# The order of the work of a linear-attention and gated-FFN kernel, laid out anew behind its first 148 entries

## The chip, the cores and the metric

The kernel runs on one core of a Trainium2 chip. The metric is the time of one execution on the device in microseconds (us). Besides the plain runs there is one profiled execution, from which all rows of the profile are.

## What is computed

Eight batches, eight heads, 576 positions, head width 64. For each batch and head the attention has no softmax: k and v are multiplied into a 64x64 matrix, q times that matrix is the output, and the output is scaled by its root mean square over the head width. The heads side by side are the 512 columns of x. Then comes a feed-forward layer with 1024 hidden columns: a ReLU, a convolution of three taps over the positions, a sigmoid of it as a gate, and a product with the output matrix.

```python
kv = np.einsum('bhsd,bhse->bhde', k, v)
out = np.einsum('bhsd,bhde->bhse', q, kv)
rms = np.sqrt(np.mean(out * out, axis=-1, keepdims=True) + 1e-06)
x = out / rms * g_norm
h = np.maximum(x @ w_in, 0.0)
# conv_out[s] = w0 * h[s - 1] + w1 * h[s] + w2 * h[s + 1], per column
out = (h * gate) @ w_out        # gate = 1 / (1 + exp(-conv_out))
```

## The kernel before, in words

All work is cut into small operations, and a list of 852 entries (ORDER) says in which order they are issued. An entry is a name with its numbers; behind an @ stands a slot: the bank of PSUM that it writes (of eight; two neighbouring banks for most), or the place in a ring of buffers in SBUF. `om.1.2.0.4@4` is the operation `om` for pair 1, row block 2, with four hidden blocks from 0 on, in bank 4. A loop at the end of the kernel runs the list from front to back, and a last pass ties each instruction to the one before it on its engine. So every engine works strictly in the list's order, and between engines only data and the reuse of banks and buffers make one wait. A bank may be written again when its last reader is done: an entry on the matmul engine (PE) with a slot may thus wait for a copy on VectorE (DVE) or ScalarE (ACT).

The work of a batch b goes like this. `Lq`, `Lk`, `Lv` load q, k and v (L348, on the queue of GpSimd, POOL). `kv` (or `kz`) multiplies k and v (L403, L480), `kva` or `kvd` copies the result to SBUF on ACT (L417) or on DVE (L415), one function with two names. `qt` transposes q on PE (L434) and `qd` copies it (L444); batches 6 and 7 are transposed by DMA instead (`tq`, L468), and `kx` moves halves of their kv matrix to the other partitions. `ot` (or `ox`) multiplies q by kv (L461, L501). For batches 0 to 3, `sq` squares it on ACT (L510), `on` or `oq` sums the squares on PE (L529, L538), `nl` takes the reciprocal root on ACT (L546), and `mo` scales on DVE into x (L557). For batches 4 to 7, `oc` copies the output to SBUF on ACT (L522), `ss` sums the squares of two batches into a few rows (L567), `ln` takes the root (L575), `sl` splits the result on DVE into parts (L582 to L585), `sp` spreads them over the partitions on PE (L594), and `mu` scales on DVE (L600).

The hidden layer is `hk`, `hs` or `hm` on PE (L659, L629, L614) with its ReLU on ACT: `rp`, `rh`, `re` (L666, L641, L620). Then `ta` makes two tap products on DVE (L682, L683), `aa` and `ab` add them (L688, L693), `sg` is the sigmoid on ACT (L699), and `mg` multiplies the gate in (L723); for four hidden blocks of batch 0, `cv` does the convolution on PE (L709) and `sc` the sigmoid (L716). `fi` are matmuls of zeros in the first 28 us. The output is `om` (`oh` for half rows) on PE (L733, L758), eight hidden blocks for a row block of 128, issued in two halves of four; `ea` copies it out of PSUM on ACT (L739), `ed` on DVE (L744), `eh` and `dh` do it for half rows, and `st` and `sh` store it from the queue of SyncE (SP).

Before an ACT operation that needs another table of functions stands a load (L228). `sg` and `sc` use one table, `nl` and `ln` the other.

The array of PE is used in several tiles: whole (128x128) for `hk`, `hs`, `hm`, `on`, `om` and `oh`, in 64x64 quarters for `kv`, `kz`, `qt`, `ot`, `ox` and `oq`, as 128x32 for `ss`, and as 32x128 for `sp`.

Of the kernel before, what the change touches and what calls it, by code (L numbers as in the profile page):

```python
# [76 lines left out]
hk.1.7.1.0@1 hk.1.5.1.1 rh.1.2.1 rh.1.0.1 rh.1.6.1 qt.2.0.0@4 rh.1.3.1 qt.2.1.0@2 Lq.5.0.4@2 sg.0.1.5 qd.2.0.0@0
sg.0.1.4 qd.2.1.0@1 ab.0.1.3 hk.1.4.1.0@6 hk.1.4.1.1 hk.1.1.0.0@7 hk.1.1.0.1 hk.1.5.0.0@4 hk.1.7.0.0@5 hk.1.0.0.0@2
hk.1.0.0.1 mg.0.1.2 rh.1.1.0 rh.1.4.1 rh.1.0.0 sg.0.1.6 ta.1.1.1@0 ta.1.1.0 aa.1.1.0 hk.1.7.1.1 hk.1.2.0.0@3
hk.1.5.0.1 hk.1.6.0.0@7 hk.1.7.0.1 hk.1.4.0.0@2 hk.1.4.0.1 hk.1.6.0.1 om.0.1.0.4@6 hk.1.2.0.1 rh.1.7.1 sg.0.1.7  # L80
rh.1.5.1 kv.2.0.2@0 rh.1.4.0 rh.1.5.0 rh.1.2.0 rh.1.6.0 kva.2.0.2@0 rh.1.7.0 om.0.2.0.4@2 mg.0.1.3 ab.1.1.0 om.0.1.4.4
# [10 lines left out]
hs.2.7.1@4 hs.3.7.0@5 qd.5.0.0@2 qd.4.1.0@3 sg.1.1.4 sg.1.1.5 hs.3.0.0@6 mg.1.1.2 ta.1.1.6@1 hs.3.3.1@0 ta.1.1.7
aa.1.1.3 hs.3.2.1@1 hs.3.2.0@7 rh.2.3.0 rh.2.6.0 rh.3.3.1 sg.1.1.3 rh.3.7.0 rh.3.2.1 rh.2.7.1 rh.3.0.0 sg.1.1.2
kv.4.0.2@2 hs.3.3.0@0 hs.3.6.0@1 kvd.4.0.2@0 ab.1.1.3 qt.5.1.0@2 ot.4.0.0@4 hs.3.0.1@6 rh.3.3.0 rh.3.2.0 rh.3.6.0
mg.1.1.1 hs.3.7.1@0 hs.3.1.0@1 hs.3.5.0@7 qd.5.1.0@4 ta.2.2.2@0 hs.3.4.0@2 om.0.7.0.4@3 sg.1.1.6 sg.1.1.7 rh.3.0.1
# [730 lines left out]
```

## Time and profile before

| | us |
|---|---|
| median of 3 runs | 177.63 |
| lowest and highest | 177.57 and 177.76 |
| the profiled execution | 177.69 |
| its span, first to last instruction | 175.8 |

The granted clock of TensorE is 0.999 of full speed in the profiled execution. PE is the matmul engine, PEld its weight loads, L733 is line 733 of the kernel. A row of a timeline has the start, the time until the last of the instructions merged in it ends, engine, line, operation and operands, and in brackets how long the engine was idle before it and what ended that. A row of the chain has start, length, and engine with what it wrote and the line. A row of stretches has the stretch, its length, and each engine's busy time in it.

### The profile page before, as it was taken

To read this page: it belongs to the slowest core of one execution; us is meant where nothing else is said; L and a number is where in the kernel's file an instruction comes from. 1 tells how busy PE (TensorE), PEld (TensorE's weight loads), DVE (VectorE), ACT (ScalarE), POOL (GpSimd) and SP (SyncE) were. 2 spreads that over 40 slices of the span, in tenths; PEclk is the share of its full clock that TensorE was granted. 3 is DMA by queue.
4 is the path that set the end of the run, shared out by engine and by line. 5 is a ranking of instruction groups with operands and counts; after the bars stand their busy time and mean duration, and the time that the engine had idled before them with its cause. 6 is when DMAs were issued, how large, how long until landed. Compare 5 with 4: busy or idle time off the path is not lost.

```text
span 175.8 us, 5059 instructions
## 1 busy us (share of the span) xinstructions
PE 168.3 (96%) x2091; PEld 100.3 (57%) x2110; DVE 146.6 (83%) x286; ACT 150.7 (86%) x272; POOL 22.5 (13%) x35
## 2 busy tenths in 40 slices
...
GB/s 162 392 321 206 207 205 208 208 208 207 208 208 210 280 209 205 128 208 232 227 240 255 60 0 0 167 121 134 60 63 0 0 20 159 123 159 181 124 190 125
DMA packets 25911, 29.10 MB, mean 165 GB/s; under 512 B 6037, under 2 KB 20385, under 8 KB 25889
## 3 DMA queue, kind: packets, MB, share of 16 engines
...
## 4 chain that ended last, share of the span: by engine, by line
PE 71%; ACT 18%; DVE 5%; DMA 3%; issue 3%; ACTq 0%
PE banks L733 30%; PE banks L629 12%; PE banks L659 8%; PE banks L614 5%; ACT taps L699 5%; ACT h L641 3%; DMA stg<-in_v_dram 3%; ACT sq L510 2%; ACT h L620 2%; PE banks L434 2%; PE banks L709 2%; PE banks L461 2%; PE banks L403 2%; PE banks L529 2%; PE banks L287 1%
## 5 line engine op out<-in xcount | busy, mean ns | idle before, releaser
L733 PE MATMUL banks<-w_out_sb,h 128*128 128x512 bf16 x265 | 62.9, 380 | 0.9 <-issue 0.3
L733 PEld LDWEIGHTS <-h 128*128 128x128 bf16 x280 | 26.1, 98 | 30.1 <-issue 1.0
L699 ACT ACTIVATE taps<-taps,cw 128x576 bf16<-128x576 bf16 (+1 forms) x44 | 40.3, 963 | 3.0 <-DVE taps L693 2.8
L629 PE MATMUL banks<-x,w_in_sb 128*128 128x288 bf16 (+2 forms) x256 | 33.8, 286 | 0.0
L641 ACT ACTIVATE h<-banks 128x288 bf16<-128x288 f32 (+2 forms) x80 | 29.5, 475 | 0.5 <-PE banks L659 0.5
L629 PEld LDWEIGHTS <-w_in_sb 128*128 128x128 bf16 x256 | 24.4, 98 | 7.1 <-issue 0.2
L723 DVE TENSOR_TENSOR h<-h,taps 128x1152 bf16<-128x1152 bf16 (+1 forms) x24 | 22.8, 952 | 1.0 <-ACT taps L699 0.9
L510 ACT ACTIVATE sq<-banks 128x576 bf16<-128x576 f32 (+2 forms) x32 | 20.7, 704 | 1.3 <-PE banks L461 1.0
L688 DVE TENSOR_TENSOR taps<-taps 128x1152 bf16<-128x1152 bf16 (+1 forms) x22 | 21.4, 974 | 0.4
L693 DVE TENSOR_TENSOR taps<-taps,h 128x1152 bf16<-128x1152 bf16 (+1 forms) x22 | 21.3, 970 | 0.2
L739 ACT ACTIVATE row<-banks 128x512 f32<-128x512 f32 x25 | 14.6, 595 | 5.1 <-issue 2.2
L682 DVE TENSOR_SCALAR taps<-h,cw 128x576 bf16<-128x576 bf16 (+1 forms) x44 | 18.8, 426 | 0.3 <-ACT h L641 0.3
L683 DVE TENSOR_SCALAR taps<-h,cw 128x576 bf16<-128x576 bf16 (+1 forms) x44 | 18.5, 421 | 0.0
L659 PE MATMUL banks<-x,w_in_sb 128*128 128x288 bf16 (+2 forms) x128 | 17.7, 286 | 0.1
L557 DVE SCALAR_TENSOR_TENSOR x<-banks,cw,rs 128x576 bf16<-128x576 f32 (+2 forms) x16 | 13.0, 814 | 5.0 <-ACT rs L546 5.0
L614 PE MATMUL banks<-x,w_in_sb 128*128 128x288 bf16 x128 | 16.7, 286 | 0.1
L614 PEld LDWEIGHTS <-w_in_sb 128*128 128x128 bf16 x128 | 12.3, 98 | 4.0
L659 PEld LDWEIGHTS <-w_in_sb 128*128 128x128 bf16 x128 | 12.2, 98 | 4.1 <-DMA w_in_sb<-in_moe_w_in_dram 0.2
L228 ACT ACT_TABLE_LOAD x10 | 12.8, 1283 | 2.0 <-issue 1.8
L444 DVE COPY qT<-banks 128x1152 bf16<-128x1152 bf16 (+2 forms) x13 | 8.7, 681 | 5.5 <-PE banks L434 5.4
L600 DVE SCALAR_TENSOR_TENSOR x<-o,cw,banks 128x576 bf16<-128x576 f32 (+2 forms) x16 | 11.9, 808 | 1.0 <-PE banks L594 1.0
L546 ACT ACTIVATE rs<-banks,eps_sb 128x576 f32<-128x576 f32 (+2 forms) x16 | 11.8, 740 | 0.7 <-PE banks L529 0.6
...
## 6 DMA issues: line engine op xcount, KB each, us to landing
...
```

Of the source, the lines that this page charges most:

```text
L510: nc.scalar.activation(T["sq", b, u, s], T["o", b, u, s], AX.Square)
L614: nc.tensor.matmul(ps[:, s, :HS], w_in_sb[:, t, f * P:(f + 1) * P], T["x", b][:, t, c0:c1], start=(t == 0), stop=(t == NT - 1))
L629: nc.tensor.matmul(ps, w_in_sb[:, t, f * P:(f + 1) * P], T["x", b][:, t, c0:c1], start=(t == 0), stop=(t == NT - 1))
L641: nc.scalar.activation(h, fr, AX.Relu)
L659: nc.tensor.matmul(T[at], w_in_sb[:, t, f * P:(f + 1) * P], T["x", b][:, t, c0:c1], start=(t == 0), stop=(t == NT - 1))
L682: nc.vector.tensor_scalar_mul(tap[:, 0, f % 2, :n, 8:8 + S], h[:, f], cw[:, f:f + 1])
L683: nc.vector.tensor_scalar_mul(tap[:, 1, f % 2, :n, :S], h[:, f], cw[:, 2 * NF + f:2 * NF + f + 1])
L688: nc.vector.tensor_add(tap[:, 1, :, :n, :S], tap[:, 0, :, :n, 7:7 + S], tap[:, 1, :, :n, 1:1 + S])
L693: nc.vector.tensor_add(y, y, span(b, n)[:, 2 * j:2 * j + 2])
L699: nc.scalar.activation(y, y, AX.Sigmoid, scale=cw[:, NF + f:NF + f + 1])
L723: nc.vector.tensor_mul(h, h, tap_of(b, j)[:, 1, :, :n, :S])
L733: nc.tensor.matmul(T["om", p, m], h[:, f, m * P:(m + 1) * P], w_out_sb[:, f, :], start=(f == 0), stop=(f == NF - 1))
```

## The change

From entry 149 on the list is laid out again. It has 852 entries as before, and nearly the same ones: `kva.2.0.2` and `kva.3.0.2` become `kvd`, the copies out of PSUM change their engine in `om.0.1`, `om.1.8`, `om.2.0` and `om.3.4` (from DVE to ACT) and in `om.1.6`, `om.1.7`, `om.3.5` and `om.3.6` (from ACT to DVE), and `eh.3.8.1` becomes `dh.3.8.1`. Most other entries move by a few places, and many get other slots. The kernel also gains operations that the list doesn't use (`ff`, `dw`, `df`, `mr`, `ad`, and `y_of` for `ad`); what `on` and `oq` write is put in one bank where both halves fit, which is so for the tiles of 256 columns of batch 0 alone.

Of the list, the parts that are spoken of:

```diff
-rh.3.1.0 sq.4.0.0@0 rh.3.5.0 rh.3.7.1 mg.1.1.3 ot.4.0.1@6 ta.2.2.0@1 ta.2.2.1 Lv.5.0.4@1 oc.4.0.0@0 Lk.5.0.4@0
-rh.3.4.0 kv.5.0.2@0 ot.4.1.0@4 om.0.7.4.4 oc.4.0.1@1 sq.4.0.1@1 kvd.5.0.2@1 ta.2.2.3 ot.5.0.0@0 ed.0.7@4 aa.2.2.1
-aa.2.2.0 ot.4.1.1@6 hs.2.7.0@2 oc.4.1.0@2 sq.4.1.0@2 ot.5.0.1@4 om.0.8.0.4@3 om.0.8.4.4 sq.5.0.0@3 oc.5.0.0@3
-sq.5.0.1@4 rh.2.7.0 oc.5.0.1@4 ot.5.1.1@0 ot.5.1.0@4 oc.4.1.1@5 sq.4.1.1@5 om.0.5.0.4@2 om.0.5.4.4 sq.5.1.1@6
-sq.5.1.0@7 ss.4.4.2@6 ss.5.4.2 ln.4@0 ab.2.2.1 ed.0.8@5 Lv.6.0.4@0 Lk.6.0.4@1 om.0.4.0.4@3 om.0.4.4.4 kz.6.0.2@6
-Lq.7.0.4@1 oc.5.1.0@6 oc.5.1.1@7 om.0.6.0.4@4 ab.2.2.0 ed.0.5@3 ea.0.4@0 sl.4@0 sg.2.2.2 sp.4.0.0.4@0 sp.4.1.1.4@2
-kvd.6.0.2@0 mu.4.1.1@2 om.0.6.4.4 sp.4.1.0.4@2 mu.4.0.0 sp.4.0.1.4@6 st.0.7 hs.2.6.1@5 mu.4.0.1 mu.4.1.0 hs.3.5.1@0
-st.0.5 ea.0.6@1 kx.6@0 sp.5.1.0.4@6 rh.2.6.1 ox.6.0.0@4 Lk.7.0.4@0 Lv.7.0.4@1 tq.6.1@0 st.0.4 st.0.3 st.0.8 st.0.6
-tq.7.0@2 tq.7.1@3 rh.3.5.1 mu.5.1.0@0 sp.5.1.1.4@0 hm.4.7@2 sp.5.0.1.4@6 mu.5.1.1 oc.6.0.0@0 sq.6.0.0@0 sp.5.0.0.4@4
...
+Lk.5.0.4@0 rh.3.1.0 rh.3.7.1 rh.3.5.0 rh.3.4.0 oc.4.0.0@0 hs.2.7.0@1 sq.4.0.0@0 ot.4.1.0@2 kv.5.0.2@4 rh.2.7.0
+ot.4.0.1@6 mg.1.1.3 om.0.7.4.4 ta.2.2.3 ta.2.2.1@1 aa.2.2.1 kvd.5.0.2@1 sq.4.1.0@1 oc.4.1.0@1 ta.2.2.0 ot.4.1.1@2
+ed.0.7@0 ot.5.0.0@4 oc.4.0.1@2 om.0.8.0.4@1 sq.4.0.1@2 om.0.8.4.4 sq.4.1.1@3 ot.5.1.1@6 aa.2.2.0 sq.5.0.0@4 oc.5.0.0@3
+ot.5.1.0@4 oc.4.1.1@4 ot.5.0.1@2 sq.5.1.1@5 om.0.5.0.4@0 om.0.5.4.4 sq.5.1.0@6 oc.5.0.1@5 sq.5.0.1@7 ss.4.4.2@2
+ss.5.4.2 ln.4@0 ab.2.2.1 om.0.4.0.4@3 om.0.4.4.4 Lv.6.0.4@0 Lk.6.0.4@1 ed.0.8@1 ab.2.2.0 ed.0.5@3 Lq.7.0.4@1
+kz.6.0.2@0 om.0.6.0.4@2 oc.5.1.0@6 oc.5.1.1@7 sl.4@0 ea.0.4@4 sp.4.1.1.4@4 sp.4.0.1.4@6 kvd.6.0.2@0 st.0.7 sg.2.2.2
+kx.6@0 om.0.6.4.4 sp.4.1.0.4@0 mu.4.0.1@2 sp.4.0.0.4@6 hs.2.6.1@3 mu.4.1.1 hs.3.5.1@4 ea.0.6@0 mu.4.1.0 ox.6.0.0@0
+rh.2.6.1 sp.5.1.1.4@2 rh.3.5.1 mu.4.0.0 sp.5.1.0.4@4 hm.4.7@6 mu.5.1.1@0 sp.5.0.0.4@2 mu.5.1.0 sq.6.0.0@0 oc.6.0.0@0
+mu.5.0.0 sp.5.0.1.4@0 sg.2.2.3 re.4.7@0 Lk.7.0.4@0 hm.4.1@4 sg.2.2.0 Lv.7.0.4@1 hm.4.0@2 hm.4.6@6 tq.6.1@0 st.0.4
...
-kvd.7.0.2@0 sq.6.1.1@1 hm.5.7@4 hm.4.5@6 ab.2.2.2 ta.2.2.6@1 ta.2.2.7 aa.2.2.3 ab.2.2.3 sq.6.1.0@2 oc.6.1.1@1
-oc.6.1.0@2 hm.5.5@2 hm.5.0@0 sg.2.2.4 re.5.7 re.4.5 om.1.2.0.4@4 re.5.0 hm.5.4@6 sg.2.2.5 re.5.5 hm.5.6@0 re.5.4
-sg.2.2.7 hm.5.2@2 sg.2.2.6 re.5.2 re.5.6 om.1.8.0.4@5 om.1.6.0.4@6 om.1.0.0.4@7 ox.7.0.0@0 kx.7@1 mg.2.2.2 ta.4.2.5@0
-ta.4.2.4 mg.2.2.3 aa.4.2.2 ox.6.0.1@2 ta.4.2.7@1 ta.4.2.6 ab.4.2.2 om.1.2.4.4 oc.7.0.0@3 oc.6.0.1@4 ea.1.2@4
-om.1.6.4.4 sq.7.0.0@3 sq.6.0.1@4 ea.1.6@3 om.1.0.4.4 ea.1.0@0 om.1.8.4.4 ox.7.1.0@0 ox.7.0.1@2 ed.1.8@2 ox.7.1.1@6
-om.1.1.0.4@4 om.1.7.0.4@5 sq.7.1.0@5 aa.4.2.3 ab.4.2.3 sq.7.0.1@6 oc.7.0.1@5 sq.7.1.1@7 ss.6.6.2@2 ss.7.6.2 ln.6@0
-om.1.7.4.4 om.1.1.4.4 om.1.4.0.4@2 ea.1.7@5 oc.7.1.0@6 ea.1.1@1 oc.7.1.1@7 st.1.2 st.1.6 st.1.0 st.1.8 sl.6@0
-om.1.4.4.4 sp.7.0.1.6@0 mu.7.0.1@0 sp.6.1.1.6@4 om.1.5.0.4@3 sp.6.0.1.6@6 sp.7.1.1.6@0 om.1.5.4.4 mu.6.1.1@1
-sp.7.0.0.6@4 ea.1.4@4 sg.4.2.5 mu.6.0.1 mu.7.1.1 sg.4.2.4 sp.7.1.0.6@6 st.1.7 st.1.1 st.1.4 sg.4.2.7 om.1.3.0.4@2
-hm.4.3@0 om.1.3.4.4 mu.7.1.0 mu.7.0.0 mg.4.2.2 ea.1.5@3 ta.4.2.1@0 ta.4.2.0 sg.4.2.6 mg.4.2.3 st.1.5 hm.4.2@4
...
+ta.2.2.5 hm.5.3@6 mg.2.2.0 aa.2.2.2 ta.2.2.7@1 ab.2.2.2 re.4.4 re.4.0 ox.6.1.1@0 re.5.1 kz.7.0.2@2 ox.6.1.0@4 re.5.3
+hm.4.5@6 sq.6.1.1@1 oc.6.1.1@1 hm.5.7@0 sq.6.1.0@2 oc.6.1.0@2 re.4.5 hm.5.5@4 sg.2.2.4 hm.5.0@6 re.5.7 ta.2.2.6
+kvd.7.0.2@0 re.5.5 om.1.2.0.4@2 hm.5.4@0 re.5.0 hm.5.2@4 sg.2.2.5 re.5.4 aa.2.2.3 ab.2.2.3 hm.5.6@6 sg.2.2.7 kx.7@1
+om.1.8.0.4@0 om.1.6.0.4@1 sg.2.2.6 om.1.0.0.4@3 re.5.2 ox.7.0.0@4 re.5.6 ox.6.0.1@6 mg.2.2.2 ta.4.2.5@0 ta.4.2.4
+mg.2.2.3 aa.4.2.2 oc.7.0.0@3 ta.4.2.7@1 ta.4.2.6 om.1.2.4.4 oc.6.0.1@4 ea.1.2@0 sq.7.0.0@3 om.1.8.4.4 om.1.0.4.4
+sq.6.0.1@4 om.1.6.4.4 ea.1.8@1 ea.1.0@2 ab.4.2.2 ox.7.0.1@4 ox.7.1.0@6 sq.7.0.1@5 ox.7.1.1@2 sq.7.1.0@6 om.1.7.0.4@0
+oc.7.0.1@5 sq.7.1.1@7 om.1.7.4.4 ss.6.6.2@4 ss.7.6.2 ln.6@0 ed.1.6@3 aa.4.2.3 ab.4.2.3 om.1.4.0.4@1 om.1.4.4.4
+oc.7.1.0@6 ed.1.7@4 oc.7.1.1@7 ea.1.4@5 sg.4.2.7 st.1.0 st.1.2 st.1.8 st.1.6 st.1.7 om.1.1.0.4@0 st.1.4 om.1.1.4.4
+ea.1.1@0 st.1.1 sg.4.2.5 sl.6@0 sp.7.0.1.6@2 sp.7.1.1.6@4 sp.6.0.1.6@6 mu.7.1.1@0 mu.7.0.1 mu.6.0.1@1 om.1.5.0.4@1
+om.1.5.4.4 sp.6.1.1.6@2 sp.7.1.0.6@4 sp.7.0.0.6@6 om.1.3.0.4@0 mu.6.1.1 mu.7.1.0 mu.7.0.0 hm.4.3@2 om.1.3.4.4 sg.4.2.4
+hm.4.2@4 ea.1.5@0 re.4.3 sg.4.2.6 ea.1.3@1 hs.6.0.1@1 hs.6.3.1@2 hs.7.6.0@3 re.4.2 rh.7.6.0@1 hs.7.7.0@0 rh.6.0.1
...
-rh.6.7.0 hs.6.3.0@1 mg.4.2.1 ab.6.1.2 om.2.6.0.4@0 om.2.6.4.4 ta.6.1.1@1 ta.6.1.0 aa.6.1.0 sg.6.1.5 om.2.3.0.4@2
...
+hs.6.7.0@0 rh.7.0.0 hs.6.3.0@1 mg.4.2.1 hs.7.6.1@3 om.2.6.0.4@6 om.2.6.4.4 rh.6.1.0 rh.6.6.0 rh.6.0.0 rh.6.7.0
...
-st.3.0 sg.7.1.5 sg.7.1.4 ed.2.0@2 om.3.4.0.4@0 om.3.5.0.4@3 st.2.0 mg.7.1.2 om.3.5.4.4 ea.3.5@5 st.3.5 om.3.4.4.4
-om.3.6.4.4 ea.3.6@1 ed.3.4@4 om.3.7.0.4@2 om.3.7.4.4 st.3.4 st.3.6 oh.3.8.1@0 ed.3.7@3 eh.3.8.1@0 st.3.7 sh.3.8.1
-oh.3.8.0@1 eh.3.8.0@2 sh.3.8.0
...
+mg.7.1.2 om.3.5.4.4 ed.3.5@0 ea.2.0@1 om.3.4.4.4 ea.3.4@2 om.3.6.4.4 om.3.7.0.4@0 st.3.0 st.3.2 om.3.7.4.4 ed.3.6@3
+st.2.0 st.3.4 st.3.5 ed.3.7@1 st.3.6 oh.3.8.1@1 st.3.7 dh.3.8.1@0 sh.3.8.1 oh.3.8.0@2 eh.3.8.0@2 sh.3.8.0
```

And of the code:

```diff
@@ def tile_transnormer_attn__then__gated_conv_ffn_kernel
+    dram = pool("dram", 1, space=bass.MemoryType.DRAM)
...
+    def pair(n):
+        if 2 * n <= 512:
+            return bank()[:, :2 * n].rearrange("p (e n) -> p e n", e=2)
+        return bank2()[:, :, :n]
...
     def kvc(eng, b, u0, n):
-        if u0 == 0:
+        if ("kvb", b) not in T:
...
     def qc(eng, b, u, s):
-        if s == 0:
+        if ("qT", b, u) not in T:
...
     def on(b, u, s):
         c0, c1 = cols(b, s)
-        ps = T["on", b, u, s] = bank2()[:, :, :c1 - c0]
+        ps = T["on", b, u, s] = pair(c1 - c0)
...
     def oq(b, u, s):
         c0, c1 = cols(b, s)
-        ps = T["on", b, u, s] = bank2()[:, :, :c1 - c0]
+        ps = T["on", b, u, s] = pair(c1 - c0)
```

More of the change, by code (lines that the diff above doesn't have):

```diff
@@ L77 @@
[L77 to L81, printed above, removed]
@@ L92 @@
[L92 to L95, printed above, removed]
-rh.3.1.0 sq.4.0.0@0 rh.3.5.0 rh.3.7.1 mg.1.1.3 ot.4.0.1@6 ta.2.2.0@1 ta.2.2.1 Lv.5.0.4@1 oc.4.0.0@0 Lk.5.0.4@0
@@ new lines @@
+hk.1.2.0.1 om.0.1.0.4@1 rh.1.5.0 sg.0.1.7 hk.1.7.0.1 hk.1.4.0.1 sg.0.1.6 rh.1.5.1 kv.2.0.2@6 mg.0.1.2 ta.1.1.1@0
+ta.1.1.0 aa.1.1.0 rh.1.7.0 ab.1.1.0 hk.1.6.0.1 om.0.2.0.4@0 rh.1.2.0 mg.0.1.3 om.0.1.4.4 rh.1.4.0 kvd.2.0.2@0
+ot.2.0.1@2 rh.1.6.0 sg.1.1.1 sg.1.1.0 ea.0.1@0 qt.3.1.0@4 sq.2.0.1@0 ta.1.1.5@1 ta.1.1.4 aa.1.1.2 om.0.2.4.4
+qd.3.1.0@2 Lv.4.0.4@0 on.2.0.1@6 Lk.4.0.4@1 nl.2.0.1@0 qt.3.0.0@4 mg.1.1.0 om.0.3.0.4@1 ea.0.2@1 qd.3.0.0@3 ot.2.1.0@4
+mo.2.0.1@0 Lq.6.0.4@0 ab.1.1.2 ot.2.1.1@6 sq.2.1.0@0 om.0.3.4.4 sq.2.1.1@1 on.2.1.0@2 ed.0.3@2 om.0.0.0.4@0 nl.2.1.0@0
@@ new lines @@
+ta.1.1.2@0 mo.2.1.0 hk.1.3.0.0@1 on.2.1.1@2 nl.2.1.1@1 om.0.0.4.4 ot.2.0.0@4 kv.3.0.2@2 hk.1.3.0.1 sq.2.0.0@0 mo.2.1.1
+on.2.0.0@6 rh.1.3.0 ed.0.0@3 kvd.3.0.2@0 hs.2.5.1@0 hs.2.0.1@1 ot.3.0.1@2 nl.2.0.0@0 ta.1.1.3 ot.3.1.1@6 rh.2.5.1@1
+rh.2.0.1 hs.2.4.1@0 hs.2.1.1@1 mo.2.0.0 hs.2.4.0@4 sq.3.0.1@0 sq.3.1.1@1 hs.2.1.0@5 aa.1.1.1 ab.1.1.1 rh.2.4.1
+rh.2.1.1 on.3.1.1@0 rh.2.4.0 hs.2.2.0@4 rh.2.1.0 hs.2.5.0@5 nl.3.1.1@0 rh.2.2.0 on.3.0.1@0 hs.2.0.0@4 rh.2.5.0
+hs.2.2.1@5 mo.3.1.1@1 ot.3.0.0@6 nl.3.0.1@1 qt.4.0.0@0 mo.3.0.1 rh.2.0.0 rh.2.2.1 ot.3.1.0@4 hs.2.3.1@2 hs.2.3.0@3
@@ L287, in fi, with ff @@
             nc.tensor.matmul(ps[:, :w], zero[:, :P], zero[:, :w], start=True, stop=True)
+    @op
+    def ff(n, w):
+        ps, z = bank(), zero.bitcast(FP32)
+        for _ in range(n):
+            nc.tensor.matmul(ps[:, :w], z[:, :P], z[:, :w], start=True, stop=True)
     @op
@@ L587, in sp, with dw, df, h_of @@
     @op
+    def dw(b0):
+        T["rd", b0] = dram.tile([P, GW], FP32, name="rd")
+        nc.sync.dma_start(out=T["rd", b0], in_=T["rs", b0])
+    @op
+    def df(b, u, s, b0):
+        w, c = width(b, s), 2 * (b - b0) + s
+        to = T["sp", b, u, s] = ring("qkv"[(4 * (b - b0) + 2 * u + s) % 3], [P, 2, 320], FP32, "spread")[:, :, :w]
+        fr = T["rd", b0].rearrange("(t c i) w -> c i t w", t=NT, i=2)[c, :, 2 * u:2 * u + 2, :w]
+        for i in range(2):
+            nc.sync.dma_start(out=to[half(i)], in_=fr[i].unsqueeze(0).to_broadcast([D, 2, w]))
+    def h_of(b, f):
+        if ("h", b // 2) not in T:
+            T["h", b // 2] = ring("h", [P, NF, 2, S], BF16, "h")
+        return T["h", b // 2][:, f, b % 2, :]
+    @op
     def sp(b, u, s, b0):
@@ L596, in sp, with mr @@
                 start=True, stop=True)
+    @op
+    def mr(b, u, s):
+        nc.vector.scalar_tensor_tensor(
+            x_part(b, u, s), T["o32", b, u, s], g_sb, T["rs", b, u, s], op0=AL.mult, op1=AL.mult)
     @op
```

77 lines of the change are left out of this document (43 added, 34 removed).

## The prediction, made before the change was run

> **What bounds the kernel now.** I read the page first, then the busy time by stretches, then the chain that ended last, then the timelines of single engines at the places where the chain changes its engine.
>
> ```profile
> span 175.8 us, 5059 instructions
> PE 168.3 (96%) x2091; PEld 100.3 (57%) x2110; DVE 146.6 (83%) x286; ACT 150.7 (86%) x272; POOL 22.5 (13%) x35
> ```
>
> ```profile
> 30.00:60.00 30.00, 29.62 (x522) 19.64 (x529) 26.39 (x52) 28.13 (x59) 6.26 (x9) 1.00 1.21 215
> 60.00:82.00 22.00, 21.55 (x418) 13.57 (x410) 19.13 (x32) 21.82 (x47) 3.93 (x5) 1.00 1.22 200
> 82.00:92.00 10.00, 9.84 (x147) 5.29 (x140) 9.21 (x15) 9.68 (x14) 0.00 (x0) 1.00 1.21 228
> 92.00:123.00 31.00, 30.72 (x293) 17.75 (x294) 29.04 (x41) 29.96 (x45) 0.00 (x0) 1.00 0.38 108
> 123.00:142.00 19.00, 18.89 (x151) 14.45 (x152) 18.82 (x27) 19.00 (x41) 0.00 (x0) 1.00 0.08 28
> 142.00:171.00 29.00, 28.89 (x134) 13.18 (x135) 24.40 (x52) 20.23 (x34) 0.00 (x0) 1.00 0.37 139
> ```
>
> The columns are PE, PEld, DVE, ACT, POOL, the granted clock (1.00 throughout) and DMA. Three engines are nearly full at once. A busy PE hides short waits, so the chain has to say who is late where:
>
> ```profile
> 79.03 0.55 ACT o L522
> ...
> 79.62 0.32 PE banks L461 x4
> ...
> 81.77 0.60 PE banks L567 x16
> ...
> 86.20 2.27 DVE x L600 x3
> ...
> 88.51 0.30 PE banks L594 x2
> ```
>
> ```profile
> 98.26 0.42 DVE kvb L415
> 98.69 1.27 DVE taps L693
> ...
> 99.98 1.25 ACT taps L699
> 101.24 1.62 ACT h L620 x3
> ...
> 108.50 0.44 PE banks L501 x8
> ```
>
> From 60 to 79.62 us ACT is on the chain; from 86.20 to 88.47 the scaling `mu` on DVE (L600) holds PE's next spread; from 98.26 to 108.50 the copy `kvd.7.0.2` and what follows it on DVE and ACT; in the rest mostly PE. So a gain on PE reaches the end only where PE is the late one.
>
> **The prices.** A change of array tile and PE's waits are read from starts of matmuls:
>
> ```profile
> 143.82 2.54 PE L733 MATMUL banks<-w_out_sb,h 128*128 128x512 bf16 x11
> ```
>
> ```profile
> 118.97 0.29 PE L594 MATMUL banks<-wparts,spread 32*128 32x256 bf16 x4
> 119.19 1.04 PE L733 MATMUL banks<-w_out_sb,h 128*128 128x512 bf16 x4
> ...
> 120.38 1.04 PE L733 MATMUL banks<-w_out_sb,h 128*128 128x512 bf16 x4
> 121.34 0.44 PE L594 MATMUL banks<-wparts,spread 32*128 32x320 bf16 x4
> ```
>
> Eleven `om` matmuls take 2.54 us with a last one of 0.38, so one follows another after (2.54 - 0.38)/10 = 0.216 us. Four of them stand between 120.38 and 121.34: 0.96 less 4 x 0.216 leaves 0.10 us for the change to the spread's 32x128 tile. From 118.97 to 119.19 are 0.22 us for a spread of 256 columns and the change back. A separate visit to another tile thus costs about 0.10 + 0.22 = 0.32 us, and spreads put together share one visit.
>
> Beside this row stands a rule of the Trainium skill, "TensorEngine Tiling (Array Packing)", Key Properties: going to another tiling mode, unlike going to another tile of the same mode, drains the TensorE. If that meant the whole 0.38 us of the last matmul before the next may start, one change would cost 0.38 - 0.216 = 0.16 us and five 0.82 us, and rival 1 below would give 177.69 - 0.82 - 0.33 = 176.5 us; the trace agrees that a change costs something, but with 0.10 us.
>
> **The change part by part.** The first 148 entries stay, so up to 30 us nothing moves. The one edit there puts both halves of two `on` tiles of 256 columns into one bank; they have the same instructions and the same reader, and I cost it at nothing. Behind them the list has 59 changes of tile in place of 64 (counted over the list's PE entries, with `kv`, `qt`, `ot`, `ox` as one tile, `sp`, `ss` and the full array as three others). At 0.10 us each that is 0.5 us of PE's time. Both lists load ten ACT tables. Where the five are:
>
> Two are near 76 us, where `hs.2.7.0` leaves its place between two `ot` groups:
>
> ```profile
> 75.95 0.44 PE L461 MATMUL banks<-qT,kvb 64*64 64x288 bf16 x8
> 76.32 0.66 PE L629 MATMUL banks<-x,w_in_sb 128*128 128x288 bf16 x4
> 77.16 0.32 PE L461 MATMUL banks<-qT,kvb 64*64 64x288 bf16 x4 [0.17 <-ACT sq L510]
> ```
>
> The `ot` at 77.16 already waits for ACT, and so does the one at 79.62. ACT does the same squares, copies and relus in both lists up to `ln.4`. In the new list `ot.5.0.1` needs bank 2 from `oc.4.1.1`, the fifth last of them, and `ss.4.4.2` needs bank 2 from `sq.5.0.1`, the very last. Worth: 0. One is near 89 us, where the three spreads of batch 5 and `ox.6.0.0` are regrouped; the next matmuls wait there for one `mu` after another, 2.27/3 = 0.76 us each. Worth: 0.
>
> The next place is 98 to 108 us. `kvd.7.0.2` goes behind `ta.2.2.7`, `ab.2.2.2` and `ta.2.2.6`, and `re.4.5` goes ahead of `sg.2.2.4`. Two waits of PE stand there now:
>
> ```profile
> 99.72 2.12 PE L614 MATMUL banks<-x,w_in_sb 128*128 128x288 bf16 x16
> 101.83 1.02 PE L733 MATMUL banks<-w_out_sb,h 128*128 128x512 bf16 x3
> ```
>
> ```profile
> 106.71 1.67 PE L733 MATMUL banks<-w_out_sb,h 128*128 128x512 bf16 x7
> 108.50 0.33 PE L501 MATMUL banks<-qT,kvb 64*64 64x320 bf16 x4
> ```
>
> Sixteen `hm` matmuls in 2.12 us, the last 0.29, follow each other after 0.122; the seventeenth was due at 99.72 + 16 x 0.122 = 101.67 and `om.1.2` came at 101.83: 0.15 us, for bank 4 from `re.5.7`. Seven `om` from 106.71 put the next at 106.71 + 7 x 0.216 + 0.10 = 108.32; `ox.7.0.0` came at 108.50: 0.18 us, for bank 0 from `re.5.6`. In the new list ACT does `re.4.5` in the 0.5 us in which DVE's copy kept `sg.2.2.4` away, so all that follows is one relu earlier, 1.62/3 = 0.54 us. Both waits are shorter than that. `om.1.2` now needs bank 2 from the moved copy, which ends after `ab` (98.69 + 1.27 = 99.96), the two products of one `ta` (2 x 0.51) and its own 0.42 (row below), at about 101.4 or, since DVE's instructions overlap a little, somewhat sooner: 0.2 us or more before PE comes at 101.67. What is late next is `mg.2.2.3`, which itself waits for `sg.2.2.6` and moves up with ACT. Worth: -0.15 - 0.18 = -0.33 us (0 if the new order meets other waits, -0.54 if PE could use ACT's whole relu). `kx.7` behind the copy starts 2.5 us later, takes
>
> ```profile
> kvx<-kvb SPq DMA_DIRECT2D x4, 32.0 KB, 3.5
> ```
>
> 3.5 us, and is first read after 112 us. POOL's queue swaps `Lv.4` and `Lk.4` only.
>
> The last two changes are near 120 us. The spreads of batches 6 and 7 go in two threes and not three twos, which saves one visit, 0.32 us. But the third spread of the second three needs banks 6 and 7 from the third `mu`:
>
> ```profile
> 116.86 0.33 DVE L582 CAST hi<-rs 128x320 bf16<-128x320 f32 x1 [0.58 <-ACT rs L575]
> ...
> 119.36 4.30 DVE L600 SCALAR_TENSOR_TENSOR x<-o,cw,banks 128x512 bf16<-128x512 f32 x6 [0.63 <-PE banks L594]
> 123.58 1.35 DVE L723 TENSOR_TENSOR h<-h,taps 128x2304 bf16<-128x2304 bf16 x1
> ```
>
> The first `mu` starts 0.39 us after the spread (118.97 to 119.36), and by 4.30/6 = 0.72 us each the third ends at most 0.39 + 3 x 0.72 = 2.55 us behind that spread. PE would be back after 0.22 + 8 x 0.216 + 0.10 = 2.05 us, so it waits up to 0.5 us. The last spread stood 121.34 - 118.97 = 2.37 us behind the first before and stands about 2.5 behind it now: the visit saved is lost, and a little more. Worth: +0.1 us (between -0.32, if `mu` were no hindrance, and +0.2).
>
> DVE's work grows by two `kvb` copies and one `dh`; `ed` and `ea` trade places with equal counts:
>
> ```profile
> L744 DVE COPY row<-banks 128x512 f32<-128x512 f32 x10 | 6.9, 685 | 4.8 <-PE banks L733 4.7
> L415 DVE CAST kvb<-banks 128x256 bf16<-128x256 f32 x4 | 1.7, 422 | 0.6 <-ACT h L620 0.5
> L682 DVE TENSOR_SCALAR taps<-h,cw 128x1152 bf16<-128x1152 bf16 x16 | 8.2, 513 | 0.0
> ```
>
> The two copies, 0.84 us, fall between 40 and 55 us; from 30 to 60 us DVE is idle for 30 - 26.39 = 3.6 us, and that hides them. Ahead of `sl.6` stand now `ed.1.6` and `ed.1.7` for `ed.1.8`, 0.69 us more; the 0.58 us in which DVE waited for `ln.6` (row 116.86) hide nearly all of it, and cost 0.1 if the waits above stay. From there DVE decides too:
>
> ```profile
> 119.36:164.64 45.28, 44.82 (x79) 1.00 0.25 92
> ```
>
> ```profile
> 139.72 1.36 DVE L723 TENSOR_TENSOR h<-h,taps 128x2304 bf16<-128x2304 bf16 x1
> ...
> 141.45 1.03 PE L733 MATMUL banks<-w_out_sb,h 128*128 128x512 bf16 x3
> ```
>
> DVE works 44.82 of 45.28 us. `om.2.6` started at 141.45 and the gate `mg.4.2.1` that it needs ended at 139.72 + 1.36 = 141.08: 0.37 us of room. If PE comes 0.23 us earlier, it still finds the gate done. At the end `mg.7.1.2` holds `om.3.5`; the new list takes `ed.2.0` from in front of it, so it keeps up. The tail behind the last matmul (one half row and its store) is the same.
>
> **Sum.** 0 (to 30 us) + 0 (76 us) + 0 (89 us) - 0.33 (98 to 108 us) + 0.1 (120 us) + 0 (behind it) = -0.23 us. The profiled execution took 177.69 us (span 175.8 and 1.9 around it), 0.06 over the median 177.63. 177.69 - 0.23 = 177.46, so I say **177.5 us**, 0.1% under the median: no change that can be told. About 0.2% (0.36 us) is what a measurement of this kernel can tell from none, so below 177.27 is faster and above 177.99 slower.
>
> **The rivals.** (1) All five changes of tile reach the end beside the two waits: -0.5 - 0.33 = -0.83, **176.9 us**. For it: PE is 96% busy. Against it: ACT is full from 60 to 82 us, and `mu` holds PE twice. (2) **Slower: DVE's chain from `sl.6` starts late.** If `ed.1.7` ends behind `ln.6`, because its `om` is late, the whole chain to `mg.7.1.2` moves with it, and behind that gate stand five more `om` groups of PE whatever happens. One eviction late is +0.69 us, **178.4 us**. It decides from the point where `sl.6` starts behind 116.86. (3) The 60 to 82 us stretch gives some back: both `ss` (L567, 0.60 us) now queue behind the last square, and only the second did before: +0.30 on -0.23, **177.8 us**. (4) The list doesn't do what it says: banks are reused sooner in the `hs` stretches (after three tiles where four stood), PE waits 0.1 to 0.2 us at several of them, the waits at 101.83 and 108.50 return elsewhere: +0.5, **178.2 us**.
>
> **Chances.** Forecast 0.36 (177.1 to 177.8; a third of it lies under 177.27), rival 1 0.20, rival 2 0.20, rival 3 0.14, rival 4 0.10. Faster: 0.20 + 0.12 = 0.32. Slower: 0.20 + 0.10 = 0.30. Same: 0.24 + 0.14 = 0.38. The range takes in rivals 1 and 2: 176.8 to 178.4.
>
> **What would show it.** Right: `om.1.2` and `ox.7.0.0` follow the matmul before without a wait; `ot` near 79.6 still waits for ACT; the second three of spreads waits for L600; `om.2.6` finds its gate done. Wrong: L582 of `sl.6` starting later than 116.86 with L744 in front of it, PE waiting at L733 for L723 near 141 or 166, or waits at L629 for L641. If the stretch to 82 us moves by more than 0.2 us either way, my reading of ACT as the bound is wrong.

## The result, and the profile after

The changed kernel took **179.22 us** (median of 6 runs, 178.93 to 179.51) beside 177.66 us for the kernel before on the same chip (6 runs, 177.57 to 177.92): a ratio of 1.0085, 95% interval 1.0071 to 1.0099. It is slower by 0.85%, or 1.56 us. I had predicted 177.5 with a range up to 178.4. The profiled execution took 179.12 us, its span is 177.3.

The page of the changed kernel, span and engines:

```profile
span 177.3 us, 5054 instructions
...
PE 168.6 (95%) x2091; PEld 100.6 (57%) x2110; DVE 148.0 (83%) x289; ACT 149.5 (84%) x269; POOL 22.3 (13%) x35
```

PE, which is on the chain for 85% of the span, works as long as before (168.6 us for 168.3); DVE works 1.4 us more and ACT 1.2 us less, by the operations that changed sides. So the loss on PE is waiting, not work. Busy time by stretches of the changed kernel, with the columns that the prediction explains:

```profile
60.00:82.00 22.00, 20.95 (x418) 13.48 (x412) 19.23 (x32) 21.75 (x47) 3.71 (x5) 1.00 1.23 197
...
92.00:123.00 31.00, 30.84 (x295) 17.90 (x297) 29.80 (x42) 30.25 (x45) 0.00 (x0) 1.00 0.37 107
...
142.00:171.00 29.00, 28.35 (x129) 12.69 (x130) 24.51 (x51) 19.89 (x34) 0.00 (x0) 1.00 0.32 120
```

From 92 to 123 us PE is fuller than before (30.84 for 30.72); from 60 to 82 us (20.95 for 21.55) and from 142 to 171 us (28.35 for 28.89) it is emptier. To see where it comes from, I set the start of the same entry on PE in each trace beside that of the trace before: its first matmul for `kz` and `ox`, its first weight load, which comes about 0.1 us ahead of the matmul, for the others (the start before in us, then the differences; e1 to e14 are the experiments below):

| entry (start before) | after | e1 | e3 | e4 | e7 | e11 | e12 | e10 | e14 |
|---|---|---|---|---|---|---|---|---|---|
| om.0.1.4.4 (43.62) | +0.18 | +0.06 | +0.21 | +0.23 | +0.11 | +0.01 | +0.09 | +0.09 | +0.09 |
| hs.2.0.0 (58.33) | -0.02 | -0.14 | +0.01 | +0.15 | -0.09 | -0.20 | -0.10 | +0.10 | +1.35 |
| on.3.1.0 (62.15) | +0.32 | +0.20 | +0.35 | +0.15 | -0.09 | -0.20 | -0.10 | +0.10 | +1.35 |
| kz.7.0.2 (96.88) | +0.28 | +0.28 | +0.14 | +0.16 | -0.08 | -0.22 | -0.12 | +0.07 | +1.36 |
| ox.7.0.0 (108.51) | -0.06 | -0.06 | -0.20 | -0.18 | -0.42 | -0.56 | -0.39 | +0.07 | +1.12 |
| om.1.3.4.4 (123.45) | -0.04 | -0.04 | -0.17 | -0.15 | -0.40 | -0.53 | -0.38 | +0.08 | +1.12 |
| om.2.1.0.4 (150.73) | +0.09 | +0.08 | -0.17 | -0.16 | -0.40 | -0.42 | -0.38 | +0.07 | +1.12 |
| om.3.1.4.4 (157.67) | +0.06 | +0.04 | -0.17 | -0.15 | -0.40 | -0.45 | -0.38 | +1.38 | +1.12 |
| oh.3.8.0 (171.60) | +0.93 | +0.11 | -0.17 | -0.15 | -0.40 | -0.38 | -0.38 | +1.38 | +1.12 |

The first row shows how far one execution lies from another: e4 and e10 have the list before up to that entry, and stand at +0.23 and +0.09. So a single difference of up to 0.2 us says little, and each column is to be read by its steps from row to row. The column "after" reads: -0.20 from 44 to 58 us, +0.34 near 60 us, -0.34 from 97 to 108 us, +0.02 to 123 us, +0.13 to 151 us, **+0.84 from 151 to 171 us**, and the span then ends 1.47 us later than before, so **+0.54 behind the last matmul group's start**. The place for which I had forecast less time is right; the two largest losses lie where I had written 0, and the one near 60 us at a place that I had not priced.

**98 to 108 us.** PE's timeline of the changed kernel:

```profile
98.01 4.11 PE L649 MATMUL banks<-x,w_in_sb 128*128 128x288 bf16 x32
101.96 1.03 PE L781 MATMUL banks<-w_out_sb,h 128*128 128x512 bf16 x3
...
105.76 2.75 PE L781 MATMUL banks<-w_out_sb,h 128*128 128x512 bf16 x12
108.44 0.33 PE L513 MATMUL banks<-qT,kvb 64*64 64x320 bf16 x4
```

By the prediction's spacings the first `om` was due at 98.01 + 32 x 0.122 = 101.91 and came at 101.96; `ox.7.0.0` was due at 105.76 + 12 x 0.216 + 0.10 = 108.45 and came at 108.44. Both waits are gone.

**151 to 172 us.** PE's timeline shows one long wait:

```profile
158.81 4.69 PE L781 MATMUL banks<-w_out_sb,h 128*128 128x512 bf16 x20
164.00 7.93 PE L781 MATMUL banks<-w_out_sb,h 128*128 128x512 bf16 x35 [0.50 <-ACT row L787]
```

In the kernel before, the chain that ended last is all but PE alone in this stretch; in the changed one it runs over ACT and DVE from 156.42 us on and comes back to PE at 164.00. Before, then after:

```profile
141.88 10.74 PE banks L733 x49
152.67 10.77 PE banks L733 x49
163.49 7.50 PE banks L733 x34
```

```profile
152.76 3.63 PE banks L781 x16
...
156.42 0.87 ACT taps L745 x2
...
163.46 0.49 ACT row L787
...
164.43 7.50 PE banks L781 x34
```

The group behind the wait is `om.2.0`. It goes to bank 0, which `ea.3.0` (ACT, L787) has to empty. Why is `ea.3.0` late? ACT's timeline:

```profile
153.01 0.60 ACT L787 ACTIVATE row<-banks 128x512 f32<-128x512 f32 x1
155.36 0.60 ACT L787 ACTIVATE row<-banks 128x512 f32<-128x512 f32 x1 [1.75 <-DMA out_dram<-row]
...
162.02 1.44 ACT L745 ACTIVATE taps<-taps,cw 128x576 bf16<-128x576 bf16 x2 [0.69 <-DVE taps L739]
163.37 0.57 ACT L787 ACTIVATE row<-banks 128x512 f32<-128x512 f32 x1
```

The row at 155.36 is `ea.2.7`. It waits 1.75 us for a **store**: it writes to place 0 of the ring of output rows, where `ea.2.8` stood, and that row is still on its way to memory. Behind it on ACT stand the two sigmoids that the next gate needs. DVE's timeline shows that gate, `mg.7.1.0`, and the last one, `mg.7.1.2`:

```profile
157.31 0.76 DVE L769 TENSOR_TENSOR h<-h,taps 128x1152 bf16<-128x1152 bf16 x1 [0.72 <-ACT taps L745]
...
166.21 0.76 DVE L769 TENSOR_TENSOR h<-h,taps 128x1152 bf16<-128x1152 bf16 x1 [0.84 <-ACT taps L745]
```

In the kernel before, `mg.7.1.0` started 0.73 us sooner:

```profile
156.58 0.75 DVE L723 TENSOR_TENSOR h<-h,taps 128x1152 bf16<-128x1152 bf16 x1
```

So the chain runs store, ACT, DVE, ACT again (162.02), `ea.3.0` at 163.37, PE. In the kernel before the same eviction, `ea.2.7`, came at 153.78 and did not wait for a store (what ended its idle time of 0.32 us is, by the profile, an instruction of ACT itself):

```profile
153.78 0.60 ACT L739 ACTIVATE row<-banks 128x512 f32<-128x512 f32 x1 [0.32 <-ACT row L739]
```

The store of `ea.2.8`, `st.2.8`, is issued at 151.3, behind `st.2.2`, and the profile gives it:

```profile
L797 SPq DMA_DIRECT2D out_dram<-row x1: 423/423/423, 151.3 to 151.3; - x1
...
DMA to landing us min/median/max: 4.0/4.0/4.0
```

4.0 us to landing, where the stores behind 140 us have a median of 2.1. That gives a first theory, **A**: the late landing of `st.2.8` is the cause of the 0.84 us. Its rival **B**: the bank is the cause, PE would wait for `ea.3.0` anyway. And **C**: the loss is made elsewhere, near 60 us and at the tail.

### The profile page after: what moved, and what is told of

It is laid out like the page before. It is cut to its first block, busy times and chain, and to the rows that moved or that the text cites. A ratio compares the mean times of both kernels' runs of the same rounds, so it can differ in the third digit from the quotient of the medians.

```text
span 177.3 us, 5054 instructions
## 1 busy us (share of the span) xinstructions
PE 168.6 (95%) x2091; PEld 100.6 (57%) x2110; DVE 148.0 (83%) x289; ACT 149.5 (84%) x269; POOL 22.3 (13%) x35
## 4 chain that ended last, share of the span: by engine, by line
PE 85%; ACT 6%; DVE 4%; issue 2%; ACTq 0%; DVEq 0%
PE banks L781 28%; PE banks L664 18%; PE banks L649 9%; PE banks L694 8%; PE banks L293 6%; PE banks L446 3%; PE banks L473 2%; PE banks L415 2%; PE banks L541 2%; PE banks L755 2%; ACT sq L522 2%; DVE x L635 1%; PE banks L624 1%; ACT o L534 1%; PE banks L806 1%
## 5 line engine op out<-in xcount | busy, mean ns | idle before, releaser
L676 ACT ACTIVATE h<-banks 128x288 bf16<-128x288 f32 (+2 forms) x80 | 28.8, 461 | 1.6 <-PE banks L694 0.8
L717 DVE TENSOR_SCALAR taps<-h,cw 128x576 bf16<-128x576 bf16 (+1 forms) x44 | 19.0, 433 | 0.0
L787 ACT ACTIVATE row<-banks 128x512 f32<-128x512 f32 x25 | 14.7, 597 | 5.2 <-issue 2.8
L718 DVE TENSOR_SCALAR taps<-h,cw 128x576 bf16<-128x576 bf16 (+1 forms) x44 | 18.8, 428 | 0.0
L293 PE MATMUL banks<-zero 128*128 128x512 bf16 x33 | 11.7, 478 | 1.4 <-DVE zero L272 1.2
```

The costliest lines, as they stand in the source:

```text
L293: nc.tensor.matmul(ps[:, :w], zero[:, :P], zero[:, :w], start=True, stop=True)
L676: nc.scalar.activation(h, fr, AX.Relu)
L717: nc.vector.tensor_scalar_mul(tap[:, 0, f % 2, :n, 8:8 + S], h[:, f], cw[:, f:f + 1])
```

## The experiments

All times are medians; each kernel was timed against the kernel before on its own chip, and the ratio (with its 95% interval) is to that. "New" is the changed kernel's list, "before" the list before. Where parts of both are put together, banks and row places are renamed so that they fit; the code around the list is the new one, and the lines of some lie one further down than in the new kernel.

### e1: another row place for ea.2.7 (new list)

```
-ea.2.7@0
+ea.2.7@5
```

> The changed kernel with one place changed: ea.2.7 writes its output row to place 5 of the ring, which is free, and not to place 0, whose last row (ea.2.8) is still being stored. Theory A (the late store holds ACT 1.75 us before ea.2.7, the gates of DVE come 0.74 us late, and ea.3.0 behind them keeps bank 0 from om.2.0): the wait of ACT for the store goes, mg.7.1.0 starts near 156.6 and not 157.3, the 0.50 us wait of PE for bank 0 goes, and the time falls by 0.6 to 0.9 us, to 178.3 to 178.6. Theory B (the bank alone is short: PE would wait for ea.3.0 however early the gates are): no change, 179.2. Theory C (the loss is made ahead of 150 us and in the stores at the very end): less than 0.2 us.

Measured: 178.25 us, ratio 1.0027 (1.0017 to 1.0038), 0.97 us under the new kernel (1.0 us by the two ratios). ACT's row for `ea.2.7`:

```profile
153.81 0.60 ACT L787 ACTIVATE row<-banks 128x512 f32<-128x512 f32 x1 [0.22 <-PE banks L781]
```

It comes 1.55 us earlier, and in the table's column e1 the loss from 151 to 172 us shrinks from 0.84 to 0.03. Theory A holds; the gain is even a little over its range.

### e2: another bank for om.2.0 (new list)

```
-om.2.0.0.4@0
+om.2.0.0.4@5
```

> The changed kernel with another place changed: om.2.0 goes to bank 5, which is free, and not to bank 0, which ea.3.0 still has to empty. Theory A: PE comes 0.66 us sooner to om.3.5.4.4, but its gate mg.7.1.2, which still ends near 166.97, holds it there (due at 163.12 + 16 x 0.216 = 166.58): a gain of about 0.2 us, 179.0. Theory B: the whole 0.66 us, 178.6.

Measured: 178.96 us, 1.0068 (1.0056 to 1.0080): 0.26 less, as theory A says. The wait for bank 0 at 164.00 is gone, but the gate `mg.7.1.2` (DVE) is as late as it was in the new kernel:

```profile
166.39 0.76 DVE L769 TENSOR_TENSOR h<-h,taps 128x1152 bf16<-128x1152 bf16 x1 [0.84 <-ACT taps L745]
```

`om.3.5.4.4`, which needs that gate, starts 1.30 us behind the group ahead of it, where 0.86 is the rule, and PE wins only a part of that back. The bank is the place where the wait shows, not where it is made. Theory B falls.

### e8: the two stores in the old order (new list)

```
-st.2.2 st.2.8
+st.2.8 st.2.2
```

> The changed kernel with one issue of SP's list moved: st.2.8 ahead of st.2.2, as in the list before; ea.2.7 stays on row place 0. Theory A says that ea.2.7 is held because st.2.8, whose row is ready early, is issued only behind st.2.2 and lands 4.0 us later. If the order of the two stores is the cause, st.2.8 is issued near 150.2, lands before 153.8, when ea.2.7 is due, and the time falls by the same 0.6 to 0.97 us as with place 5, to 178.2 to 178.5. If the landing itself is what is slow (instruction packets of 16 and 8 KB pass at 152 to 154 us in both kernels), a part of the wait stays and the time falls by less than 0.5 us: 178.7 or more.

Measured: 178.28 us, 1.0023 (1.0014 to 1.0032), the same as e1, although `ea.2.7` stays on place 0. The store's row in the trace:

```profile
L797 SPq DMA_DIRECT2D out_dram<-row x1: 332/332/332, 150.1 to 150.1; - x1
...
DMA to landing us min/median/max: 2.0/2.0/2.0
```

Issued at 150.1 it lands after 2.0 us. The store that is now second, `st.2.2` at 150.9, takes 3.9 us; so does `st.2.2` in the kernel before, at the same place. In all 16 traces the last store issued between 150.5 and 152.1 us is slow (3.8 to 4.9 us), and in some the one ahead of it too; what the new list changes is which row that is, and whether anybody waits for it.

### e10: the collision alone (before)

```
+st.2.2 st.2.8
-ea.2.7@2
+ea.2.7@4
...
-st.2.8 st.2.2
```

> The kernel before, with only the collision of the new list put in: st.2.2 issued ahead of st.2.8, and ea.2.7 on the row place that ea.2.8 has just used (place 4). Theory A: ea.2.7 waits for the landing of st.2.8 to about 155.3 and not 153.8, the gates behind it come 0.7 us late; PE has bank 2 for om.2.0 there, so only the gates count: 0.3 to 0.9 us slower, 178.1 to 178.7. If the loss of the new list needs the rest of its order as well: within 0.2 us of 177.8.

Measured: 178.75 us, 1.0049 (1.0031 to 1.0067): 0.95 us slower. ACT and PE of this kernel:

```profile
155.94 0.60 ACT L788 ACTIVATE row<-banks 128x512 f32<-128x512 f32 x1 [2.40 <-DMA out_dram<-row]
```

```profile
158.40 3.83 PE L782 MATMUL banks<-w_out_sb,h 128*128 128x512 bf16 x17 [1.17 <-ACT row L788]
```

One row place and the order of two stores are enough for a loss of that size. The profiled execution was the slowest of the six (179.27 us, the others 178.16 to 178.80), so its waits are longer than those of the median; its store took 4.5 us. Here PE is not held by the gates, as I had expected, but already by the next eviction that queues behind `ea.2.7` and two sigmoids on ACT.

### e3 and e4: the parts of the list by themselves

```
e3: new[:630]    + before[630:]
e4: before[:444] + new[444:630] + before[630:]
```

> The changed kernel's list for its first 630 entries (to about 125 us), and from there the list before, banks and row places renamed so that they fit. Theories A and B (all of the loss lies behind that point): the time of the kernel before, 177.4 to 177.8. Theory C (the loss of 0.28 us at 58 to 82 us reaches the end): 178.0 or more.

> The list before, with only entries 444 to 630 (about 80 to 125 us) of the new list: the move of kvd.7.0.2 and re.4.5, the spreads in two threes. My forecast of -0.33 + 0.1 for these places: 177.4 where before is 177.66. If DVE's chain of gates behind 119 us takes the gain back: 177.6 to 177.7. If the gain needs the new start: no gain and no loss.

Measured: e3 177.57 us, 0.9985 (0.9976 to 0.9993); e4 177.76 us, 0.9998 (0.9989 to 1.0006). e3 shows that everything over 177.8 us is lost behind entry 630. e4's matmuls gain 0.34 us from 97 to 108 us (column e4: +0.16 to -0.18), but its time is that of before within 0.15 us: my -0.33 stands in the trace and isn't shown in the time.

### e5, e6, e9, e13: the tail

Behind e1 there were 0.4 us left over before. I looked at three differences in the tail (theory D: the packet costs, and the operation on DVE brings it in early; theory E: stores issued close behind one another cost): `dh.3.8.1` on DVE for `eh.3.8.1` on ACT, `st.3.4` ahead of `st.3.5`, and an 8 KB packet of kind "instruction" that runs while the last half row is stored. Packets of e1 behind 173.2 us:

```profile
q1 hardware_dynamic: 348, 0.35, 37.6%
q14 instruction: 1, 0.01, 0.7%
...
out_dram<-row SPq DMA_DIRECT2D x1, 128.0 KB, 2.2
```

The two half rows of the kernel before, with the median of the time until they have landed:

```profile
out_dram<-row SPq DMA_DIRECT2D x2, 128.0 KB, 1.7
```

```
e5: e1 with  -dh.3.8.1@0          +eh.3.8.1@0
e6: e1 with  -st.3.4 st.3.5       +st.3.5 st.3.4
e9: e1 with  st.0.0 (53 us) issued as four stores of 32 rows
e13: before with  -st.3.5 ... st.3.4   +st.3.4 st.3.5
```

> The changed kernel with ea.2.7 on row place 5, and the first half of the last row copied by ACT again (eh.3.8.1), not by DVE (dh.3.8.1). What is left over the kernel before (178.25 against 177.83) is to lie in the last store: its packets end 1.75 us after the issue, 1.35 before, and an instruction packet of 8 KB passes in those same microseconds (173.77); in the kernel before such a packet comes only at 177.59, behind the end. Theory D (the packet holds one engine's last ten packets up, and DVE's one instruction more brings it in early): without dh it leaves the last store, and the time falls by about 0.4 us, to 177.8. Theory E (the three stores that SP issues at 169.23, 169.66 and 170.14 crowd the last ones): no change, 178.2.

> The changed kernel with ea.2.7 on row place 5, and st.3.5 issued ahead of st.3.4 as in the list before, dh kept. Theory D: no change, 178.2, and the 8 KB packet still lies in the last store. Theory E: the stores no longer bunch, the last one lands 0.4 us sooner, 177.8.

> The changed kernel with ea.2.7 on row place 5, as in the first experiment (178.25, 1.0027 of before), and the first store, st.0.0 at 53 us, issued as four of 32 rows each: three more issues in SP's program, at a place where nothing waits for them. The late tail order is kept, so SP's three stores still bunch near 169 to 170 us. In the lists with that order the 8 KB instruction packet came 0.42 us behind the issue of the very last store; with the mended order it came behind st.3.7, two issues earlier, and 0.46 us went. Theory D2 (what costs is the packet in the last store, and it comes at a place of SP's own program): three more issues bring it in about three issues earlier, ahead of the last stores; the time falls to 177.8 although the stores bunch. Theory E (the bunching costs): 178.25, unchanged.

> The kernel before with one issue of SP's list moved: st.3.5 behind st.3.4, so that the last three whole rows are stored in the new kernel's order and bunch (near 169.2, 169.6 and 170.1 us in place of 168.25, 169.16 and 169.98). Theory E (the bunched stores push the last one back): 0.4 us slower, 178.2, whatever the instruction packets do. Theory D3 (the loss is the 8 KB packet that runs inside the last store; the order of the stores only decides when it comes): 0.4 us slower if the trace shows that packet near 173.6, and no change, 177.8, if it stays behind the end as in the kernel before (177.59).

Measured: e5 178.28 us, 1.0027 (1.0015 to 1.0039), no change: the engine of the half row is not it, and that part of theory D falls. **e6 177.79 us, 0.9995 (0.9986 to 1.0004): the order of two stores is worth 0.46 us** (0.49 beside e5, timed on the same chip). Its packets behind 173.2 us:

```profile
q1 hardware_dynamic: 346, 0.35, 36.4%
...
out_dram<-row SPq DMA_DIRECT2D x1, 128.0 KB, 1.7
```

The last half row lands 0.5 us sooner, and the instruction packet isn't among them: it came at 172.33, ahead of the half rows, not at 173.77. e13 tells the two theories apart: the new order of the stores in the kernel before gives 177.92 us, 1.0006 (0.9998 to 1.0015), 0.14 us and not 0.4. There the stores bunch, the packet stays behind the end, and the last store lands after 1.7 us:

```profile
q1 hardware_dynamic: 337, 0.33, 34.3%
...
out_dram<-row SPq DMA_DIRECT2D x1, 128.0 KB, 1.7
```

So bunching (theory E) costs little, and the loss goes with the packet. In all 16 traces the two go together: with the packet inside, the last store's packets end 1.74 to 1.75 us behind its issue, without it 1.34 to 1.35. In e1 nine packets of 1 KB follow one another from 174.70 to 175.04, when all the others of the two half rows have gone: a part of a store is late, not the whole. No run takes the packet out and leaves all else, so that it is the cause is inferred. What decides when the packet comes stays **open**: three more issues on SP (e9) did not move it (173.81), and the order of two stores did. So theory D2 of e9's expectation falls. e9 was even slower than e1, 178.60 us, 1.0041 (1.0028 to 1.0054). Its trace shows why: SP ends with a fixed row of waits, one semaphore after another, 0.06 us each. In e1 the semaphores of the last two stores come near the end of that row and two steps follow the last landing (175.56 to 175.69); in e9 they come near its front, and seven follow (175.59 to 176.02).

### e7, e11, e12, e14: 30 to 80 us

```
e7:  new[:305] + before[305:444] + new[444:630] + before[630:]
e11: new with entries 305 to 444 from before, ea.2.7@5, st.3.5 ahead of st.3.4
e12: new[:305] + before[305:]
e14: before with  -kva.2.0.2@0 +kvd.2.0.2@0,  -kva.3.0.2@0 +kvd.3.0.2@0
```

> The new list to entry 305 (about 50 us), the list before from there to 444 (about 80 us), the new one from 444 to 630, the list before from there to the end. In the traces the new order loses about 0.3 us near 60 us, where hs.2.3.0 goes ahead of on.3.0.0, and gains 0.34 us at 98 to 108 us. If the first is a loss that reaches the end, this is 0.2 us or more below the list with the old end alone (177.57): 177.3. If the stretch from 60 to 82 us ends at ACT's time whatever PE does at 60 us: 177.5 to 177.6, the same.

> The changed kernel with three places mended: ea.2.7 on row place 5, st.3.5 issued ahead of st.3.4, and entries 305 to 444 (about 50 to 80 us) in the old order. If the three losses are separate and add up: 177.79 (the first two) less 0.2 to 0.36 us for the third: 177.4 to 177.6, as fast as or faster than before by 0.2 per cent. If they cover one another: 177.8.

> The list before, with only the entries 148 to 305 (about 30 to 50 us) of the new one. The list with this and the new middle took 177.38. If the middle (98 to 108 us) is worth the 0.31 us that its matmuls show in the trace: 177.6 to 177.7 here, since only the middle is taken out. If the gain is made near 47 us, where the traces of the new start come 0.2 us nearer to the old ones: 177.4.

> The kernel before with the one change of engine that lies in the stretch from 30 to 50 us: the two kvb copies of batches 2 and 3 go from ACT to DVE (kva to kvd), at their old places in the list. The list with all of the new order from 30 to 50 us took 177.27, 0.31 per cent under before. If the gain there is ACT's relief of two copies: 177.3 to 177.5. If it comes from the order of the entries (PE's transposes qt.3.0.0 take 0.48 us in place of 0.70, since they no longer wait in their midst): 177.8, or more if DVE is late for it. My prediction had these two copies at nothing.

Measured: e7 177.38 us, 0.9975 (0.9966 to 0.9984). e11 177.43 us, 0.9978 (0.9970 to 0.9987), 0.36 under e6: the three losses are separate and add up. **e12 177.27 us, 0.9969 (0.9957 to 0.9981)**, the lowest median of all; the intervals of e7, e11 and e12 overlap. e14 178.91 us, 1.0061 (1.0047 to 1.0075).

Near 60 us the loss is one relu. ACT in the new kernel, then in e7:

```profile
61.08 0.89 ACT L676 ACTIVATE h<-banks 128x288 bf16<-128x288 f32 x2
...
61.87 0.73 ACT L558 ACTIVATE rs<-banks,eps_sb 128x576 f32<-128x576 f32 x1
```

```profile
61.22 0.42 ACT L677 ACTIVATE h<-banks 128x288 bf16<-128x288 f32 x1
61.52 0.76 ACT L559 ACTIVATE rs<-banks,eps_sb 128x576 f32<-128x576 f32 x1
```

With `hs.2.3.0` ahead of `on.3.0.0`, ACT does `rh.2.3.0` ahead of `nl.3.0.0` too: two relus where one stood, and the norm comes 0.3 us later.

e14 is the surprise. The two copies that go from ACT to DVE cost 1.1 us at their old places. PE's timeline of e14:

```profile
47.07 0.40 PE L542 MATMUL banks<-sq,ones 128*128 128x288 bf16 x2 [0.54 <-ACT sq L523]
...
54.85 1.14 PE L665 MATMUL banks<-x,w_in_sb 128*128 128x288 bf16 x8 [0.50 <-DVE kvb L428]
```

e12 has the same copies on DVE and is 0.5 us faster than before, so the new order of 30 to 50 us makes up for that cost; no run has the new order with the copies on ACT, and what they cost in it is not shown. Part of e12's gain is made at 98 to 108 us, with the old list there:

```profile
101.53 1.03 PE L782 MATMUL banks<-w_out_sb,h 128*128 128x512 bf16 x4
...
105.33 2.75 PE L782 MATMUL banks<-w_out_sb,h 128*128 128x512 bf16 x12
108.12 0.33 PE L514 MATMUL banks<-qT,kvb 64*64 64x320 bf16 x4
```

Here `ox.7.0.0` comes at 105.33 + 12 x 0.216 + 0.10 = 108.02, within 0.1: the waits that I wanted the moved copy to take away are nearly gone without moving it. `kvd.7.0.2` starts 0.36 us sooner beside its neighbours than in the trace before. e14 does so too and gains 0.24 us here (+1.36 to +1.12), while e10, with the copies on ACT, gains nothing (+0.07 to +0.07): this part goes with the engine of the two copies, not with the order of the entries. Why stays open. So e12 and e7, whose intervals overlap, leave nothing that the moved middle adds on top of the new start.

## Why the prediction was wrong, point by point

- **"0 (behind it)" failed, and it is the largest part of the miss.** I followed PE's banks and the gates, and wrote that "the new list takes `ed.2.0` from in front of it, so it keeps up". I didn't follow the third thing an eviction needs, a free place for its row, and so not the order of the stores that free them. What the runs showed in its place: `ea.2.7` waits 1.75 us for the landing of `st.2.8`, and the gates and `ea.3.0` behind it come late. e1, e8 and e10 put that at 0.94 to 0.97 us.
- **"The tail behind the last matmul (one half row and its store) is the same" failed.** Which engine copies the half row makes no difference (e5), but the last store isn't the same: +0.54 us in the trace, 0.46 of it by the order of `st.3.4` and `st.3.5` (e6). It goes with an instruction packet that then falls into the last store; that the packet is the cause is inferred.
- **"0 (76 us)" and "0 (89 us)" held by their mechanism**: the changes of tile there gave nothing. But the stretch lost 0.3 us near 60 us, at a place that I hadn't looked at, more than the 0.2 us that I had set as the sign of a wrong reading. ACT is the late engine there, as I read it; that the new list puts one relu more ahead of a norm, I didn't see. Rival 3 had this size and put it at the `ss` groups.
- **"-0.33 (98 to 108 us)" was right in the trace**, -0.34, with both waits gone. In the time it isn't shown (e4), and with another start it comes without the move (e12).
- **"+0.1 (120 us)" was a little too much**: +0.02. PE waits for the third `mu` as I said. `sl.6` starts at 116.80 behind its `ed` (116.20), so rival 2, DVE late from `sl.6`, did not come, although its 178.4 us lay nearest:

```profile
116.20 0.68 DVE L792 COPY row<-banks 128x512 f32<-128x512 f32 x1
116.80 0.32 DVE L594 CAST hi<-rs 128x320 bf16<-128x320 f32 x1
```

- **The cover of 3.6 us of idle DVE for the two `kvb` copies was a wrong reason.** Idle time in a stretch hides a copy only if it lies where the copy stands: at the old places the same copies cost 1.1 us (e14). That the new order to 50 us gains as a whole, 0.31% (e12), I hadn't forecast either.
- **Rival 4** (banks reused sooner, PE waits) is what PE's row at 164.00 looks like, though its 178.2 us are 1 us short. But it named the `hs` tiles, and e2 shows that the bank alone is worth 0.26 us.

The five changes of tile cannot be seen in any of this: e12, whose list behind entry 305 is the old one and so has none of them, has the lowest median. That e11, with the three losses mended, ends at 177.43 us beside my 177.46 is luck: its gain goes with the new start, which the sum had at 0.
